# A fused attention and two-layer mixture kernel: where the block means are placed from, which banks the second queries use, and who copies the last transposed weights

## The chip, the cores and the metric

The kernel runs on one core of one Trainium2 chip. The metric is device time in microseconds (us) of one execution. Three runs of the kernel before took 491.3, 493.27 and 496.1 us, the median is 493.27. One execution was profiled.

## The reference, cut to what matters

```python
# q, k, v: (2, 8, 768, 64) float32
block, window = (32, 16)
k_sum = k.reshape(B, H, nb, block, D).max(axis=3)     # 24 block maxima per head
v_sum = v.reshape(B, H, nb, block, D).mean(axis=3)    # 24 block means per head
scores_l = scale * np.matmul(q, k.transpose(0, 1, 3, 2))
scores_s = scale * np.einsum('bhsd,bhnd->bhsn', q, k_sum) + np.log(block)
scores_l_m = np.where(np.abs(pos[:, None] - pos[None, :]) < window, scores_l, -1e9)
a = softmax(np.concatenate([scores_l_m, scores_s], axis=-1))
attn = np.matmul(a, np.concatenate([v, v_sum], axis=2))
x = attn.transpose(0, 2, 1, 3).reshape(B * S, H * D)  # 1536 x 512
h = x @ w_in; x = (h * np.cos(h)) @ w_out             # 512 -> 2048 -> 512
h = x @ w_in2; solu = h * softmax(h)                  # 512 -> 1024
out = layernorm(solu) * g_ln @ w_out2                 # 1024 -> 512
```

## The kernel before, in words

The program has three stages. The first is the attention, some 103 us; the two feed-forward parts follow and are long runs of matmuls. The order of every engine's work is written out by hand: what the Python code emits first runs first on its engine.

The attention goes over 8 pairs of heads, each cut into 3 groups of 4 query tiles, 24 groups in all. `step` counts from 0 to 28, and each stage of a group lags behind the scores: in step s, TensorE makes the scores of group s+1 (`emit_s`, tile `sps`, L510), transposes the softmax weights of group s-4 (`emit_t`, tile `aps`, L547) and multiplies them with the values of group s-5 (`emit_av`, tile `ops`, L565). ScalarE takes the exponential of group s-1 (L530), copies the transposed weights to SBUF (`emit_at`, tile `at`, L555; from group 20 on VectorE does it, L553) and copies the products into `X` (L579; VectorE from group 19, L577). VectorE finds the row maxima (L521) and sums, GpSimd subtracts and normalizes (L525, L540).

For each pair the keys and queries are loaded (`kt`, `qt`), laid side by side (`kg`, `qg`), transposed by TensorE (L443, L482) into one PSUM tile `qk`, and read out: block maxima by VectorE (`ksum`, L455), key windows by ScalarE (`kx`, L464, then the ends, L471 and L474, one step later), scaled queries by ScalarE (`qx`, L496). Pair 0 is different: its queries go into banks 2 and 3 (tiles `q0`, `q1`), which are not yet needed, and VectorE scales them out of there in two halves (L492).

The values of a pair are loaded in four DMAs (`vt`, L389 and L393). The block means are made on the chip: TensorE sums blocks (`sum_v`, tile `vsum`, L421), ScalarE scales the sum (`scale_v`, tile `vm`, L429), and two DMAs place it into rows 96 to 119 of `vt` for all 12 tiles (`place_vsum`, L436). The first product of the pair needs both placings. `VSUM_AT` says in which step a pair's means are summed; the placing is issued a step later, by SyncE (SP), which issues all loads too. Two or three weight tiles of the feed-forward part are prepared during the attention (loads `raw`, L163, L164, L171, L186, L187).

In the program, each DMA takes one of eight completion semaphores, in turn over all issuing engines, and before it is issued it waits for the last transfer that had the same one.

From step 24 on (`drain`), the first hidden tiles of the feed-forward part run through ScalarE and VectorE (L243, L248, L253, L258, L263, L264) between the last groups of the attention. Their products `y` (L276) follow the last `ops`.

Of the kernel before, what the change touches and what calls it, by code (L numbers as in the profile page):

```python
# [34 lines left out]
def fused_kernel(  # L35
# [14 lines left out]
    nc = tc.nc  # L50
# [43 lines left out]
    WSTEPS = (4, 7, 10, 13, 16, 19, 20, 21)  # L94
    XS = (7, 10, 13, 16)
    IDLE = (0, 0, 0)
    DVE_AT = 20
    DVE_X = 19
    DVE_NORM = 99
    LAST = 5  # L100
# [225 lines left out]
    def drain(k):  # L326

        if k == 0:
            table(AF.Sin)
        for stage, at in STAGES:  # L330
            if 0 <= k - at < GF and (stage, k - at) != (emit_g, GF - 1):
                stage(k - at)


    def attention():
        st = ExitStack()
        with st:
# [24 lines left out]
            def load_q(n):  # L362
                q_t[n] = load_heads(q, n, "qt", NR)

            def load_k(n):
                k_t[n] = load_heads(k, n, "kt", 2)
# [17 lines left out]
            def load_v(n):  # L384
                b, hp = divmod(n, NP)
                t = io.tile([P, NT, 2, D], F32, tag="vt", name="vt", bufs=4)
                for j in range(2):
                    o = v[b, 2 * hp + j].offset
                    nc.sync.dma_start(  # L389
                        out=t[0:WIN, 1:NT - 1, j, :],  # L390
                        in_=bass.AP(v.tensor, o + (QT - BAND) * D, [[D, WIN], [QT * D, NT - 2], [1, D]]),
                    )
                    nc.sync.dma_start(  # L393
                        out=t[0:WIN, 0:NT:NT - 1, j, :],
                        in_=bass.AP(v.tensor, o, [[D, WIN], [(S - WIN) * D, 2], [1, D]]),
                    )
                v_t[n] = t
# [29 lines left out]
            def scale_v(n):  # L427
                m = io.tile([P, 2 * D], F32, tag="vm", name="vm")
                nc.scalar.activation(out=m, in_=vs_t[n], func=AF.Copy, scale=1.0 / BLOCK)  # L429
                vs_t[n] = m  # L430

            def place_vsum(n):
                m = vs_t.pop(n)
                for c in range(2):
                    at = WIN + c * NS // 2
                    nc.sync.dma_start(  # L436
                        out=v_t[n][at:at + NS // 2].rearrange("p t j d -> p t (j d)"),
                        in_=m[D * c:D * c + NS // 2].unsqueeze(1).to_broadcast([NS // 2, NT, 2 * D]))

# [35 lines left out]
                    out=kx[:, :, WIN:KW], in_=ks_t.pop(n).unsqueeze(1).to_broadcast([P, NT, NS]), func=AF.Copy)  # L475

            def emit_q(n):
                if n == 0:
                    qk_t["q", n] = bank(2, "q0"), bank(3, "q1")
                t, (a, b) = q_t.pop(n), qk_t["q", n]  # L480
                for c in range(NR):
                    nc.tensor.transpose(  # L482
                        (a, b)[c // (NR // 2)][:, (c % (NR // 2)) * P:(c % (NR // 2) + 1) * P],
                        t[:, c].rearrange("p h d -> p (h d)"), ident)

            def emit_qx(n):
                qx = io.tile([P, S], F32, tag="qx", name="qx")
                rows = qx.rearrange("p (i r) -> p i r", r=NR)
                src = qk_t.pop(("q", n))
                if n == 0:  # L490
                    for r in range(2):
                        nc.vector.tensor_scalar_mul(  # L492
                            rows[:, :, r * NR // 2:(r + 1) * NR // 2],
                            src[r][:, 0:S // 2].rearrange("p (r i) -> p i r", i=P), 0.125)
                else:
                    nc.scalar.activation(  # L496
                        out=rows, in_=strided(src[0], 0, [[1, P], [P, NR]]), func=AF.Copy, scale=0.125)
                kx_t["q", n] = qx
# [50 lines left out]

            def emit_at(G):  # L550
                at = sm_p.tile([KW, NG, P], F32, tag="at", name="at", bufs=2)
                if G >= DVE_AT:
                    nc.vector.tensor_copy(at, at_t[G])  # L553
                else:
                    nc.scalar.activation(out=at, in_=at_t[G], func=AF.Copy)  # L555
                at_t[G] = at

            def emit_av(G):
# [27 lines left out]
            nc.sync.dma_start(out=mask.rearrange("p t k -> p (t k)"), in_=c_mask)  # L586
            load_k(1)
            load_q(1)
            load_k(2)
            load_q(2)  # L590
            load_v(0)
            nc.gpsimd.memset(small, 0.0)
            nc.gpsimd.memset(strip, 0.0)
            warm_up(8)
# [12 lines left out]


            LX, LN, LT, LA = 1, 2, 4, 5
            VSUM_AT = {3: 0, 4: 1, 7: 2, 9: 3, 12: 4, 13: 5, 16: 6, 19: 7}  # L610
            VLOAD_AT = {1: 1, 4: 2, 6: 3, 8: 4, 10: 5, 13: 6, 16: 7}
            for step in range(NGR + LA):
                n, g = divmod(step, GPP)
# [34 lines left out]
                    emit_max(step)  # L648
                if step == 1:
                    emit_ksum(ahead)  # L650
                drain(step - NGR)
                if LT <= step < NGR + LT:
                    emit_at(step - LT)
                weights.finish()
                if summed:
                    emit_norm(step - LN)
# [3 lines left out]
                    emit_kx(ahead)  # L660
                if step == 1:
                    emit_kx_ends(1)
                if step == 0:
                    emit_qx(1)
                if g == 2 and n + 2 < NPAIR:
                    emit_qx(n + 2)
# [13 lines left out]
                    load_q(n + 3)  # L680
                if step in VLOAD_AT:
                    load_v(VLOAD_AT[step])
                if step - 1 in VSUM_AT:
                    place_vsum(VSUM_AT[step - 1])
                if step in VSUM_AT:
                    scale_v(VSUM_AT[step])

    with tc.manual_schedule():

# [300 lines left out]
```

## Time and profile before

| | us |
|---|---|
| runs (3) | 491.3, 493.27, 496.1 |
| the profiled execution | 493.17 |
| its span, first to last instruction | 491.4 |
| TensorE busy | 479.3 (98%) |
| ScalarE busy | 313.6 (64%) |
| VectorE busy | 303.0 (62%) |
| GpSimd busy | 152.6 (31%) |

The profiled execution is 0.1 us off the median of the runs; 1.8 us lie around its span. Shares are means over stages: from 103.5 us to the end TensorE runs without a gap to speak of, and what can change is in front of that.

### The profile page before, as it was taken

Reading aid. Unit: us, or ns where it says so; the run is one execution under the profiler, and the core shown is the slowest. Engines: PE = TensorE matmul, PEld = TensorE weight load, DVE = VectorE, ACT = ScalarE, POOL = GpSimd, SP = SyncE. Lnnn points to the kernel's source line nnn. Section 1 sums busy time; section 2 is a strip of 40 time slices with the busy share of each in tenths; the row PEclk is TensorE's granted clock in tenths of the full one; section 3 lists DMA queues with packets and bytes.
Section 4 is the critical chain, followed back from the end, with each engine's and each line's share of the span. In section 5 each row is a group of like instructions: output and inputs, shape, how many; then the busy total and the mean of one; then the engine's idle time right before and its main releaser. Section 6 shows DMA issues by size and latency. Waiting matters only on the chain.

```text
span 491.4 us, 7884 instructions
## 1 busy us (share of the span) xinstructions
PE 479.3 (98%) x2943; PEld 394.5 (80%) x2943; DVE 303.0 (62%) x666; ACT 313.6 (64%) x539; POOL 152.6 (31%) x146
## 2 busy tenths in 40 slices
PE   8789999899999999999999999999999999999997
PEld 5668887678888888888888888888888888888886
DVE  3668976883445446556474655556477776776661
ACT  3669878756685766556655653788624867777621
POOL 3469977722432222222222220245500011110000
PEclk9889999999999999999999999999999999999999
DMA  8987854201222322332223220220001333223211
GB/s 258 285 199 210 212 135 127 87 2 43 87 85 90 122 88 87 92 122 88 87 91 120 88 86 27 94 96 0 0 2 43 87 90 83 65 64 65 69 40 43
DMA packets 59046, 46.17 MB, mean 94 GB/s; under 512 B 40448, under 2 KB 51328, under 8 KB 59008
## 3 DMA queue, kind: packets, MB, share of 16 engines
q1 hardware_dynamic: 59008, 45.67, 32.4%
q8 instruction: 23, 0.38, 0.3%
q14 instruction: 15, 0.12, 0.1%
HBM read 36.61 MB, written 3.15 MB: 81 GB/s over the span
## 4 chain that ended last, share of the span: by engine, by line
PE 88%; SPq 5%; POOL 2%; DVE 1%; ACT 1%; issue 1%; DMA 1%
PE y L276 27%; PE h L234 25%; PE o L865 13%; PE h L751 13%; PE sps L510 3%; SPq L393 3%; PE ops L565 2%; PE aps L547 2%; PE vsum L421 2%; SPq L357 1%; SPq L389 1%; POOL sm L525 1%; PE tp L799 1%; DMA vt<-vm 1%; POOL sm L540 1%
## 5 line engine op out<-in xcount | busy, mean ns | idle before, releaser
L234 PE MATMUL h<-xs,w 128*128 128x512 f32 x576 | 141.2, 391 | 0.0
L276 PE MATMUL y<-gs,w 128*128 128x512 f32 x576 | 138.1, 389 | 0.0
L276 PEld LDWEIGHTS y<-gs,w 128*128 128x128 f32 x576 | 108.1, 188 | 22.4
L234 PEld LDWEIGHTS h<-xs,w 128*128 128x128 f32 x576 | 107.2, 188 | 21.6
L187 POOL TENSOR_TENSOR w<-s,w 128x512 fp32r<-128x512 f32 x48 | 62.2, 1295 | 164.9 <-ACT w L186 141.9
L243 ACT ACTIVATE r<-h 128x512 int32<-128x512 f32 x48 | 28.7, 597 | 85.9 <-PE h L234 85.9
L248 DVE SCALAR_TENSOR_TENSOR r<-r,h 128x512 f32<-128x512 int32 x48 | 33.0, 687 | 67.4 <-ACT r L243 67.3
L865 PE MATMUL o<-w,ls 128*128 128x512 f32 (+1 forms) x312 | 67.8, 373 | 0.0
L751 PE MATMUL h<-w,xs 128*128 128x512 f32 x288 | 67.6, 390 | 0.0
L171 DVE SCALAR_TENSOR_TENSOR s<-raw 128x512 int32<-128x512 int32 x48 | 37.9, 790 | 44.8 <-ACT raw L164 38.3
L865 PEld LDWEIGHTS o<-w,ls 128*128 128x128 f32 x312 | 55.3, 188 | 10.7 <-DVE ls L841 0.4
L751 PEld LDWEIGHTS h<-w,xs 128*128 128x128 f32 x288 | 53.9, 188 | 11.1
L786 POOL TENSOR_TENSOR st<-st,mhalf 128x1 f32<-128x1 f32 x12 | 6.6, 550 | 110.1 <-DVE st L785 101.7
L204 POOL TENSOR_TENSOR xs<-X,xs 128x512 fp32r<-128x512 f32 x22 | 29.6, 1353 | 32.7 <-ACT xs L203 32.7
L253 ACT ACTIVATE r<-r,half_pi 128x512 f32<-128x512 f32 x48 | 34.5, 718 | 1.3 <-DVE r L248 1.3
L264 DVE TENSOR_TENSOR gs<-h,gs 128x512 fp32r<-128x512 f32 x48 | 32.6, 680 | 4.2 <-ACT gs L263 4.0
L258 DVE TENSOR_TENSOR h<-h,r 128x512 f32<-128x512 f32 x48 | 32.9, 686 | 0.4 <-ACT r L253 0.4
L163 ACT ACTIVATE raw<-raw 128x512 f32<-128x512 f32 x48 | 31.9, 664 | 0.0
L164 ACT ACTIVATE raw<-raw 128x512 int32<-128x512 uint32 x48 | 31.8, 663 | 0.0
L186 ACT ACTIVATE w<-s 128x512 fp32r<-128x512 f32 x48 | 30.1, 626 | 1.2 <-DVE s L171 0.9
L768 ACT ACTIVATE e<-h,st 128x1024 f32<-128x1024 f32 (+1 forms) x13 | 13.6, 1049 | 26.6 <-DVE st L764 23.1
L525 POOL TENSOR_TENSOR sm<-sm,mx 128x480 f32<-128x480 f32 x24 | 26.1, 1090 | 9.8 <-DVE mx L521 9.5
(81 smaller groups left out, 570.3 us busy)
## 6 DMA issues: line engine op xcount, KB each, us to landing
raw<-in_moe_w_in_dram SPq DMA_DIRECT2D x24, 512.0 KB, 3.6
raw<-in_moe_w_out_dram SPq DMA_DIRECT2D x24, 512.0 KB, 3.3
vt<-in_v_dram SPq DMA_DIRECT2D x16, 240.0 KB, 3.5
kt<-in_k_dram SPq DMA_DIRECT2D x8, 384.0 KB
qt<-in_q_dram SPq DMA_DIRECT2D x8, 384.0 KB, 7.7
out_dram<-osb SPq DMA_DIRECT2D x11, 256.0 KB, 2.0
vt<-vm SPq DMA_DIRECT2D x16, 72.0 KB
vt<-in_v_dram SPq DMA_DIRECT2D x16, 48.0 KB, 4.1
```

Of the source, the lines that this page charges most:

```text
L163: nc.scalar.activation(out=hw, in_=hw, func=AF.Prelu, scale=REBIAS, alpha=NEGATIVE)
L164: nc.scalar.activation(out=lw, in_=lw.bitcast(U32), func=AF.Copy, scale=TOP3)
L171: nc.vector.scalar_tensor_tensor(out=self.f32[i], in0=t[:, :, 1], scalar=3, in1=t[:, :, 0], op0=ALU.logical_shift_left, op1=ALU.bitwise_or)
L187: nc.gpsimd.tensor_tensor(out=w[:, 1, :], in0=f, in1=as32(w[:, 0, :]), op=ALU.subtract)
L234: nc.tensor.matmul(h, lhsT=w[:, a, f * P:(f + 1) * P], rhs=xs_of[tb, c][:, b_, :], start=(m == 0), stop=(m == 3 * KC - 1))
L248: nc.vector.scalar_tensor_tensor(out=r, in0=r.bitcast(I32), scalar=TWO_PI, in1=h_of[step], op0=ALU.mult, op1=ALU.subtract)
L253: nc.scalar.activation(out=r, in_=r, func=AF.Sin, scale=-1.0, bias=half_pi)
L258: nc.vector.tensor_tensor(out=h, in0=h, in1=r, op=ALU.mult)
L264: nc.vector.tensor_tensor(out=gs[:, 1, :], in0=r, in1=as32(gs[:, 0, :]), op=ALU.subtract)
L276: nc.tensor.matmul(y[e], lhsT=w[:, a, e * P:(e + 1) * P], rhs=gs[:, b_, :], start=(f == 0 and i == 0), stop=(f == GF - 1 and i == 2))
L751: nc.tensor.matmul(banks[n], lhsT=xs_of[NTB + t // TPB, c][:, a, t0:t0 + P], rhs=weights.done[w2i[c][n]][:, b_, :], start=(m == 0), stop=( ...
L865: nc.tensor.matmul(o, lhsT=ls_of[t][f // 4][:, a, s0:s0 + P], rhs=w[:, b_, cols], start=(f == 0 and i == 0), stop=(f == NF2 - 1 and i == 2))
```

## The change

Three things. The queries of pair 1 go into banks 2 and 3 like those of pair 0, and VectorE scales them. The placing of the block means is issued from ScalarE's queue, right behind the scaling and in the same step; for pair 0 the sum is moved from step 3 to step 1 and its load ahead of the loads of pair 2. In steps 24 to 27 ScalarE copies the transposed weights instead of VectorE, and `emit_at` stands ahead of `drain`.

```diff
@@ -94,7 +94,6 @@
-    DVE_AT = 20
@@ -433,7 +432,7 @@
                 for c in range(2):
                     at = WIN + c * NS // 2
-                    nc.sync.dma_start(
+                    nc.scalar.dma_start(
                         out=v_t[n][at:at + NS // 2].rearrange("p t j d -> p t (j d)"),
@@ -475,7 +474,7 @@
             def emit_q(n):
-                if n == 0:
+                if n < 2:
                     qk_t["q", n] = bank(2, "q0"), bank(3, "q1")
@@ -487,7 +486,7 @@
                 src = qk_t.pop(("q", n))
-                if n == 0:
+                if n < 2:
                     for r in range(2):
@@ -549,10 +548,7 @@
                 at = sm_p.tile([KW, NG, P], F32, tag="at", name="at", bufs=2)
-                if G >= DVE_AT:
-                    nc.vector.tensor_copy(at, at_t[G])
-                else:
-                    nc.scalar.activation(out=at, in_=at_t[G], func=AF.Copy)
+                nc.scalar.activation(out=at, in_=at_t[G], func=AF.Copy)
@@ -586,9 +582,9 @@
             load_k(1)
             load_q(1)
+            load_v(0)
             load_k(2)
             load_q(2)
-            load_v(0)
@@ -607,7 +603,7 @@
-            VSUM_AT = {3: 0, 4: 1, 7: 2, 9: 3, 12: 4, 13: 5, 16: 6, 19: 7}
+            VSUM_AT = {1: 0, 4: 1, 7: 2, 9: 3, 12: 4, 13: 5, 16: 6, 19: 7}
@@ -648,9 +644,9 @@
-                drain(step - NGR)
                 if LT <= step < NGR + LT:
                     emit_at(step - LT)
+                drain(step - NGR)
                 weights.finish()
@@ -660,7 +656,6 @@
                 if step == 1:
                     emit_kx_ends(1)
-                if step == 0:
                     emit_qx(1)
@@ -680,10 +675,9 @@
-                if step - 1 in VSUM_AT:
-                    place_vsum(VSUM_AT[step - 1])
                 if step in VSUM_AT:
                     scale_v(VSUM_AT[step])
+                    place_vsum(VSUM_AT[step])
```

ScalarE's order from step 2 to the start of step 5, before (`sm` is an exponential, in place; `kx`, `qx`, `at` and `vm` as above):

```order
L530 ACTIVATE sm1_98<-sm1_98 128x4x120
L496 ACTIVATE qx_292<-qk_268 128x768
L530 ACTIVATE sm2_99<-sm2_99 128x4x120
L464 ACTIVATE kx_331<-qk_268 128x10x2x48
L429 ACTIVATE vm_333<-vsum_305 128x128
L530 ACTIVATE sm3_100<-sm3_100 128x4x120
L471 ACTIVATE kx_331<-qk_268 128x2x2x48
L474 ACTIVATE kx_331<-ksum_322 128x12x24
L555 ACTIVATE at_374<-aps_344 120x512
L429 ACTIVATE vm_395<-vsum_349 128x128
L530 ACTIVATE sm4_101<-sm4_101 128x4x120
```

And of the change, with what each row waits for (DMAHW is one of the eight semaphores; the last transfer that had DMAHW6 is the load of `kt` of pair 4):

```order
L529 ACTIVATE sm1_98<-sm1_98 128x4x120 [waits Pool_49]
L495 ACTIVATE qx_312<-qk_288 128x768 [waits PE_49]
L529 ACTIVATE sm2_99<-sm2_99 128x4x120 [waits Pool_49]
L463 ACTIVATE kx_338<-qk_288 128x10x2x48 [waits DVE_49]
L529 ACTIVATE sm3_100<-sm3_100 128x4x120 [waits Pool_49]
L470 ACTIVATE kx_338<-qk_288 128x2x2x48
L473 ACTIVATE kx_338<-ksum_329 128x12x24
L551 ACTIVATE at_379<-aps_349 120x512 [waits PE_49]
L428 ACTIVATE vm_398<-vsum_354 128x128 [waits PE_49]
L435 DMA vt_270<-vm_398 12x12x128 [waits DMAHW3_49,Activation_49]
L435 DMA vt_270<-vm_398 12x12x128 [waits DMAHW6_49]
L529 ACTIVATE sm4_101<-sm4_101 128x4x120 [waits Pool_49]
```

The scaling for pair 0 has moved out of this piece into step 1, ahead of the first row. Behind each of the eight scalings stand two DMAs now, and behind them the exponential of the next step.

TensorE's order from step 0 to step 4, before (`qk` by keys `kg` and queries `qg`):

```order
L443 MATMUL qk_209<-ident_73,kg_199 128x128 x6
L482 MATMUL qk_209<-ident_73,qg_207 128x128 x6
L510 MATMUL sps_224<-kx_167,qx_171 64x120 x8
L510 MATMUL sps_259<-kx_242,qx_222 64x120 x8
L443 MATMUL qk_268<-ident_73,kg_246 128x128 x6
L482 MATMUL qk_268<-ident_73,qg_248 128x128 x6
L510 MATMUL sps_296<-kx_242,qx_222 64x120 x8
L421 MATMUL vsum_305<-vt_125,strip_110 64x128 x12
L510 MATMUL sps_335<-kx_242,qx_222 64x120 x8
L547 MATMUL aps_344<-ident_73,sm0_97 120x128 x4
L421 MATMUL vsum_349<-vt_254,strip_110 64x128 x12
```

And of the change:

```order
L442 MATMUL qk_209<-ident_73,kg_199 128x128 x6
L481 MATMUL q0_216<-ident_73,qg_207 128x128 x3
L481 MATMUL q1_217<-ident_73,qg_207 128x128 x3
L509 MATMUL sps_224<-kx_167,qx_171 64x120 x8
L420 MATMUL vsum_233<-vt_121,strip_110 64x128 x12
L509 MATMUL sps_279<-kx_255,qx_259 64x120 x8
L442 MATMUL qk_288<-ident_73,kg_262 128x128 x6
L481 MATMUL qk_288<-ident_73,qg_264 128x128 x6
L509 MATMUL sps_316<-kx_255,qx_259 64x120 x8
L509 MATMUL sps_340<-kx_255,qx_259 64x120 x8
L546 MATMUL aps_349<-ident_73,sm0_97 120x128 x4
L420 MATMUL vsum_354<-vt_270,strip_110 64x128 x12
```

The first block sums stand in front of the fourth scores, and the queries of pair 1 no longer share a tile with its keys.

ScalarE's order in steps 24 to 27, of the change (before, the four `at` rows were VectorE's, and the first `r` stood right behind `small`):

```order
L529 ACTIVATE sm5_102<-sm5_102 128x4x120
L551 ACTIVATE at_1492<-aps_1470 120x512
L321 ACT_TABLE_LOAD
L321 ACTIVATE small_74<-small_74 128x1
L551 ACTIVATE at_1518<-aps_1497 120x512
L242 ACTIVATE r_1520<-h_1015 128x512
L551 ACTIVATE at_1544<-aps_1525 120x512
L252 ACTIVATE r_1520<-r_1520,half_pi_76 128x512
L242 ACTIVATE r_1548<-h_1305 128x512
L262 ACTIVATE gs_1551<-h_1015 128x512
L551 ACTIVATE at_1573<-aps_1555 120x512
```

Two copies now stand ahead of the first `r` or right behind it.

## Rows read from the trace of the kernel before

**Rows 1.** Windows: us, busy of each engine (instructions), granted clock, DMA share, GB/s.

```profile
20.00:25.43 5.43, 5.43 (x86) 4.60 (x84) 5.21 (x21) 3.79 (x10) 3.40 (x4) 0.98 1.07 347
25.43:79.31 53.88, 51.53 (x762) 43.46 (x759) 44.33 (x179) 42.71 (x91) 45.67 (x40) 0.97 0.72 184
103.49:491.00 387.51, 384.71 (x1732) 318.99 (x1728) 225.98 (x375) 241.56 (x397) 82.97 (x70) 1.00 0.24 71
```

**Rows 2.** Chain that ended last: start us, us, what.

```profile
14.41 3.36 SPq L393
...
23.42 2.58 SPq L393
...
27.15 2.90 DMA vt<-vm
```

**Rows 3.** TensorE timeline: start us, us, engine line op tiles [idle before <-releaser].

```profile
15.66 1.04 PE L510 MATMUL sps<-kx,qx 64*64 64x120 f32 x16 [2.54 <-ACT kx L474]
...
17.82 1.49 PE L482 MATMUL qk<-ident,qg 128*128 128x128 f32 x6
...
20.67 1.53 PE L421 MATMUL vsum<-vt,strip 96*64 96x128 f32 x24
22.13 1.04 PE L510 MATMUL sps<-kx,qx 64*64 64x120 f32 x16
...
30.19 0.92 PE L565 MATMUL ops<-at,vt 120*64 120x64 f32 x16 [2.12 <-DMA vt<-vm]
```

**Rows 4.** VectorE and ScalarE timelines in the head, pairs 0 to 2.

```profile
7.66 1.02 DVE L492 TENSOR_SCALAR qx<-q 128x384 f32<-128x384 f32 x2 [0.50 <-PE q L482]
...
9.58 0.84 ACT L373 ACTIVATE qg<-qt 128x768 f32<-128x768 f32 x1 [0.81 <-DMA qt<-in_q_dram]
...
13.03 0.96 DVE L455 TENSOR_REDUCE ksum<-qk 128x24 f32<-128x768 f32 x1 [1.40 <-ACT qx L496]
...
19.34 0.81 ACT L496 ACTIVATE qx<-qk 128x768 f32<-128x768 f32 x1 [3.25 <-PE qk L482]
...
25.26 0.28 ACT L429 ACTIVATE vm<-vsum 128x128 f32<-128x128 f32 x1 [0.57 <-PE vsum L421]
25.43 0.59 ACT L530 ACTIVATE sm<-sm 128x480 f32<-128x480 f32 x1
```

**Rows 5.** Windows around TensorE's two idle stretches (third last number: granted clock).

```profile
18.00:20.00 2.00, 2.00 (x15) 1.67 (x15) 0.00 (x0) 0.66 (x1) 0.49 (x1) 0.50 0.71 163
...
30.00:32.00 2.00, 1.81 (x26) 1.73 (x28) 0.00 (x0) 0.86 (x2) 0.00 (x0) 0.62 0.89 159
32.00:34.00 2.00, 2.00 (x18) 1.36 (x16) 1.74 (x10) 1.23 (x3) 1.18 (x1) 0.53 1.15 225
```

**Rows 6.** Tile vm and kt, min/median/max ns; SyncE timeline of one pair.

```profile
L436 SPq DMA_DIRECT2D vt<-vm x16: 778/786/997, 26.1 to 80.3; - x16
...
L357 SPq DMA_DIRECT2D kt<-in_k_dram x8: 379/438/722, 0.7 to 51.8; - x8
...
40.07 1.66 SPq L436 DMA_DIRECT2D vt<-vm  x2
```

**Rows 7.** ScalarE timeline: waits in the steady part.

```profile
31.14 0.38 ACT L579 ACTIVATE X<-ops 128x256 f32<-128x256 f32 x1 [3.49 <-PE ops L565]
...
79.14 0.28 ACT L429 ACTIVATE vm<-vsum 128x128 f32<-128x128 f32 x1 [0.63 <-PE vsum L421]
...
82.25 0.38 ACT L579 ACTIVATE X<-ops 128x256 f32<-128x256 f32 x1 [0.74 <-PE ops L565]
```

**Rows 8.** Waits (us in total, times, longest us), then timelines of the drain.

```profile
PE aps L547 <- DVE at L553: 1.6, 2, 0.9
...
101.71 0.68 DVE L553 COPY at<-aps 120x512 f32<-120x512 f32 x1
102.31 0.41 DVE L577 COPY X<-ops 128x256 f32<-128x256 f32 x1
...
94.70 0.58 ACT L243 ACTIVATE r<-h 128x512 int32<-128x512 f32 x1
```

## The prediction, made before the changed kernel ran

> **What bounds the kernel now.** I read the windows first. From 103.5 us to the end TensorE is busy 384.7 of 387.5 us at the full granted clock [rows 1]. Nothing of the change lies there, so every microsecond has to come out of the 103.5 us in front, and it counts only as far as the first `y` starts earlier. The chain of waits, read second, is all SyncE in the head: loads being issued, some of them very slowly (3.36 and 2.58 us for one issue), then the placings, and 2.90 us until the needed ones have landed [rows 2]. That landing releases the first product of pair 0: TensorE starts it at 30.19 after 2.12 us of waiting [rows 3]. In the head TensorE waits once more, 2.54 us until 15.66, for the key windows of pair 1 [rows 3]. After each of the two waits the clock falls: granted 0.50 at 18 to 20 us, 0.62 and 0.53 at 30 to 34 us [rows 5], so for most of this time it is the lower of its two levels, 1.2 GHz.
>
> From there to 79.3 us TensorE is busy 51.5 of 53.9 us; ScalarE is busy 42.7, GpSimd 45.7, VectorE 44.3 [rows 1] (the window runs from ScalarE's exponential of group 4 to that of group 19). So TensorE sets the pace there, and ScalarE has 11.2 us of waiting, the largest part for products of TensorE (3.49 us in one place [rows 7]). These 11.2 us are what the new work on ScalarE has to fit into.
>
> **The head, step by step.** (a) The block maxima of pair 1 started at 13.03 after 1.40 us of waiting for ScalarE's `qx`, which reads the same tile [rows 4]. With queries in banks of their own this wait goes: VectorE, free at 11.6, finishes `ksum` at 12.6 (0.96 us, against 14.0). VectorE then pays 1.02 us for the two halves of `qx`, as it did for pair 0 [rows 4]; ScalarE loses one `qx` of 0.81 us. The key windows, which released the scores at 15.66, end some 1.3 us earlier, about 14.3. (b) In front of the fourth scores now stand the block sums, which run from 13.1, where the idle stretch began (15.66 - 2.54), for 1.5 us [rows 3]. So the scores start at 14.6 instead of 15.66, and TensorE's idle stretch is filled. The values of pair 0 must be there by 13.1. They are 0.6 MB (2 x 240 and 2 x 48 KB) and now follow the load of pair 1, of which ScalarE used the last part at 9.6 [rows 4]; at 347 GB/s [rows 1] that is 1.7 us more, at 163 [rows 5] 3.5, so between 11.3 and 13.1. The keys and queries of pair 2 land as much later in exchange, about when VectorE gets to them. (c) ScalarE scales at 14.6 and issues two DMAs. No row shows a DMA issued by ScalarE. The same two on SyncE took 1.66 us, 0.78 to 1.00 each [rows 6]; that is the nearest row, and I take it, with 0.15 us more, since the row behind `vm` no longer starts 0.11 us before its end [rows 4] and the DMA waits for that end: **1.8 us a pair of placings**. The bounds are 0.76 us (two of SyncE's cheapest issue, 0.38 [rows 6]) and 5 us (two of its slow ones [rows 2]). They end at 16.7 and the exponential behind them at 17.3. The next `qx` needs TensorE's queries: 1.0 us of scores, two transposes of 0.75 each (one took 1.49 at half the clock [rows 3]), so 17.1. It starts at 17.3 against 19.34 [rows 4] and is hardly held by the DMAs. (d) Before, the scores of group 5 started 2.8 us after that `qx` and the scaling of pair 1 3.1 us after these scores (19.34, 22.13, 25.26 [rows 3, 4]). Now: 20.1 and 23.2. Then 0.3 us of scaling, 1.8 us of DMAs, and the exponential of group 4 starts at **25.2, before 25.43: -0.2 us**. TensorE reaches the first product near 26 instead of 30.19, since its placing landed long before. TensorE has won 4 us, ScalarE nearly nothing.
>
> **The steady part.** Now ScalarE is behind, and its sum decides. From the exponential at 25.43 to the one at 79.31 it did 42.7 us of work [rows 1, 7]. Six pairs of placings stand in this stretch (pairs 2 to 7): 6 x 1.8 = 10.8. Of the old 11.2 us of waiting I keep 0.8: the waits for products disappear where TensorE is ahead, the 0.63 us for the last block sum [rows 7] stays, since its scores hang on ScalarE's own `qx`. Sum 54.3 against 53.88: **+0.4**. The next wait for a product, 0.74 us at 82.25 [rows 7], absorbs **0.7**, and GpSimd's chain behind it follows ScalarE. Until step 21 that makes -0.2 + 0.4 - 0.7 = -0.5.
>
> **The rest.** SyncE is relieved of 16 issues, which cost nothing: its loads come well ahead of their use after 30 us, so neither that nor their order buys time. Lower bound nothing, upper bound nothing, except for the keys of pair 4, below. In the drain TensorE waited twice for VectorE's copies, 1.6 us in all [rows 8]. These waits go, but the first `r` on ScalarE, at 94.70, then stands behind two copies more (0.6 us each, one of them in a gap), about 1.0 us later. VectorE's `X` hangs on that chain, in whose rounds it saves a copy, 0.60 us from start to start. The last `X` that releases a product starts at 102.31 [rows 8] + 1.0 - 2 x 0.6 + 0.2 of new waiting for ScalarE = 102.3, and the last product follows it as before. I take **-0.15**; the bounds are -1.6 (both waits gone) and +1.0 (the late `r` in full).
>
> **Sum:** -0.5 - 0.15 = -0.65, on 493.17 of the profiled execution, which is 0.1 from the median: **492.5 us**. An exchange, not a gain: 4 us that TensorE wins in the head are spent on 12.6 us of issues on ScalarE.
>
> **The page that disagrees.** The rows say 0.78 us of the issuing engine for one placing. The Trainium skill, "DMA: Bandwidth & Descriptors", gives about 50 ns for the sequencer's part of a DMA (section "Anatomy of one DMA — SWDGE (gpsimd) path", so for another issuing path), and says under "Issuing engines are not separate DMA queues" that issuing is usually small beside the transfer. By it the seven pairs would cost 0.7 us and the time would be that of the first rival. This trace does not agree, with 0.78 us.
>
> **Rivals.**
> 1. *ScalarE hardly pays for the issue.* For it: SyncE issues other DMAs in 0.38 us [rows 6]. Against it: all 16 placings took at least 0.778 there. At 0.76 us a pair the seven after the first are 7 us cheaper, more than TensorE can use: it would be the bound again, with its 4.2 us of earlier start and the 1.7 us that the lower clock cost it after 30.19 (2 x 0.38 + 2 x 0.47 [rows 5]). Time 493.2 - 5.9 = 487.3; with part of it, up to 489.5. Chance 0.2.
> 2. *Slower: the DMA holds ScalarE's queue.* ScalarE works in order, and a DMA that can't go out stops everything behind it. Two things may hold it: the issue itself stalls while loads crowd the engines, as SyncE's did for 3.36 us at 14.41 and 2.58 at 23.42 [rows 2], exactly where the first two placings now stand; or the semaphore's last transfer has not landed, for pair 1 the keys of pair 4, which queue behind two weight tiles. For it: the DMA share is 1.07 at 20 to 25 us [rows 1]. Against it: later placings on SyncE took 1.66 us [rows 6], and the share is 0.72. Price: holding the first two for 2 to 3 us puts the exponential of group 4 to 27 to 29, +2 to +4, so 495 to 497; if later ones are held by 1 us each as well, 500. It decides from the point where a pair costs more than 1.9 us on average: each 0.1 us more is 0.7 us of time. Chance 0.25.
> 3. *The clock falls once more.* In my times TensorE has 1.5 to 2 us of waiting before 20 us, for the maxima. After 2.54 and 2.12 us it fell to 1.2 GHz [rows 3, 5]. At half speed the scores, transposes and sums before the second scaling take 1.5 us longer: 494. Chance 0.2, inside the range.
> 4. *The change doesn't do what it says:* the drain's copies shift the wait to VectorE's `X` and lose up to 1 us, the early sum waits for its load. 493.5; chance 0.1, not told from the forecast.
>
> That leaves 0.25 for the sum as it stands.
>
> **How the numbers follow.** Forecast with cases 3 and 4: 0.55, from 491 to 494.5. Case 1: 487 to 489.5. Case 2: 494.5 to 500. The range 488 to 497.5 leaves out half of case 1 and the far end of case 2. One per cent, about what a measurement of this kernel can tell from no change, is 4.9 us: faster than 488.3 is two thirds of case 1 (0.14), slower than 498.2 a third of case 2 and some unknown (0.11), the rest within.
>
> **What would show it.** In the changed profile: ScalarE's exponential of group 4 near 25.2; the first product near 26 without a wait for `vt<-vm`; gaps of 1.8 us behind seven `vm` rows; ScalarE's waits for `ops` nearly gone until 72 us and TensorE's idle time spread over the steady part instead; the exponential at 79.31 shifted by -0.5 to +1; the last product at 102.7. It is wrong if a pair of issues costs much under 1.5 or over 2.2 us, or if TensorE and not ScalarE still paces the part after 30 us.

## The result and the profile after

The changed kernel takes 496.56 us in the median of 18 runs (494.99 to 499.57), the kernel before, beside it, 493.23 (491.3 to 496.1). The ratio is 1.0072 with a 95% interval of 1.0052 to 1.0092: 0.7% slower, where no change was forecast. The profiled execution took 496.0 us with a span of 494.2; before it was 493.17 and 491.4.

| starts at, us | before | after | difference |
|---|---|---|---|
| exponential of group 4 (ScalarE) | 25.43 | 27.30 | +1.87 |
| exponential of group 19 | 79.31 | 82.73 | +3.42 |
| first `y` (TensorE) | 103.49 | 106.27 | +2.78 |

The 2.78 us are the whole 2.8 by which the span grew (387.9 us lie between the first `y` and the end in both): nothing changed behind the first `y`. The profiled execution lies 0.6 us under the median of the runs. ScalarE's timeline in the head, and around the last pair of placings (start us, us, engine line op tiles [idle before <-releaser]; ACTq is ScalarE's DMA queue being issued):

```profile
14.74 0.28 ACT L428 ACTIVATE vm<-vsum 128x128 f32<-128x128 f32 x1 [0.51 <-PE vsum L420]
15.05 2.23 ACTq L435 DMA_DIRECT2D vt<-vm  x2
17.33 0.60 ACT L529 ACTIVATE sm<-sm 128x480 f32<-128x480 f32 x1 [2.31 <-DMA vt<-vm]
17.84 0.79 ACT L495 ACTIVATE qx<-qk 128x768 f32<-128x768 f32 x1
...
25.32 0.28 ACT L428 ACTIVATE vm<-vsum 128x128 f32<-128x128 f32 x1 [1.48 <-PE vsum L420]
25.63 1.62 ACTq L435 DMA_DIRECT2D vt<-vm  x2
27.30 0.60 ACT L529 ACTIVATE sm<-sm 128x480 f32<-128x480 f32 x1 [1.70 <-DMA vt<-vm]
...
81.06 1.62 ACTq L435 DMA_DIRECT2D vt<-vm  x2
82.73 0.61 ACT L529 ACTIVATE sm<-sm 128x480 f32<-128x480 f32 x1 [1.70 <-DMA vt<-vm]
...
84.83 0.37 ACT L575 ACTIVATE X<-ops 128x256 f32<-128x256 f32 x1
```

Each pair of placings stands alone on ScalarE: 0.31 us after the scaling begins the issue begins, and the exponential behind it starts after 1.7 to 2.0 us without work, 2.31 us at the first pair. The trace names the transfer as releaser, but the exponential reads nothing that it wrote, and it starts 0.05 us after the last issue ends (15.05 + 2.23 and 17.33, 25.63 + 1.62 and 27.30): ScalarE's order held it. The wait of 0.74 us for a product at 82.25 [rows 7] is gone.

What the late exponential at 17.33 does, on VectorE, then on TensorE:

```profile
17.96 0.66 DVE L533 TENSOR_REDUCE ss<-sm 128x4 f32<-128x484 f32 x1 [1.25 <-ACT sm L529]
```

```profile
20.63 1.54 PE L509 MATMUL sps<-kx,qx 64*64 64x120 f32 x16 [2.54 <-DVE mx L520]
22.10 1.11 PE L546 MATMUL aps<-ident,sm 128*120 128x128 f32 x4
23.14 2.13 PE L420 MATMUL vsum<-vt,strip 96*64 96x128 f32 x24
25.20 1.04 PE L509 MATMUL sps<-kx,qx 64*64 64x120 f32 x16
...
28.06 0.69 PE L561 MATMUL ops<-at,vt 120*64 120x64 f32 x16
```

The sum waits for it, the maxima stand behind the sum and the block maxima on VectorE, and TensorE waits 2.54 us for the maxima. The scores, transposes and block sums behind that take 1.54, 1.11 and 2.13 us where they took 1.04, 0.65 and 1.53 at the full clock; the scaling of pair 1 waits for these sums until 25.32. The first product no longer waits for its placing and starts at 28.06 instead of 30.19 [rows 3]. By windows (us, busy time of PE, PEld, DVE, ACT and POOL, granted clock, DMA share, GB/s):

```profile
20.00:22.00 2.00, 1.37 (x16) 1.20 (x16) 1.97 (x17) 1.16 (x2) 1.44 (x2) 0.75 0.97 336
22.00:24.00 2.00, 2.00 (x14) 1.56 (x14) 2.00 (x4) 1.33 (x4) 2.00 (x3) 0.50 1.00 336
24.00:26.00 2.00, 2.00 (x36) 1.83 (x32) 1.69 (x11) 0.28 (x1) 1.20 (x2) 0.90 1.14 335
...
27.30:82.73 55.43, 50.21 (x755) 42.16 (x754) 40.79 (x168) 42.55 (x91) 43.20 (x40) 1.00 0.68 173
82.73:106.27 23.54, 19.93 (x239) 14.72 (x238) 16.19 (x50) 19.74 (x38) 12.47 (x13) 1.00 0.26 74
106.27:494.00 387.73, 384.75 (x1731) 319.03 (x1728) 225.73 (x375) 241.40 (x396) 83.00 (x70) 1.00 0.24 71
```

The stretch between the two exponentials, 53.88 us before [rows 1], takes 55.43, though TensorE has less to do in it at the full clock (the half clock at 30 to 34 us [rows 5] is gone). ScalarE's work is the same, 42.55; its waits between 26 and 80 us (us in total, times, longest us) say where the rest is:

```profile
ACT sm L529 <- POOL xs L203: 5.4, 3, 2.0
ACT sm L529 <- POOL sm L539: 3.4, 2, 1.7
ACT sm L529 <- DMA vt<-vm: 1.7, 1, 1.7
ACT X L575 <- PE ops L561: 0.8, 3, 0.3
```

The first three lines are six pairs, 10.5 us: the releaser is whatever ended last by the profile, but each of the six lies behind an issue of 1.62 to 1.90 us. (This window has pair 1's wait in it and leaves out the last pair's; both are 1.70, so the six pairs between the two exponentials come to 10.5 us as well.) The waits for products, 8.6 us before, are down to 0.8. ScalarE sets the pace now.

### The profile page after: what moved, and what is told of

Read it like the earlier page. It is cut to its first block, busy times and chain, and to the rows that moved or that the text cites. A ratio compares the mean times of both kernels' runs of the same rounds, so it can differ in the third digit from the quotient of the medians.

```text
span 494.2 us, 7882 instructions
## 1 busy us (share of the span) xinstructions
PE 477.2 (97%) x2943; PEld 392.5 (79%) x2943; DVE 299.7 (61%) x664; ACT 314.7 (64%) x542; POOL 150.9 (31%) x146
## 4 chain that ended last, share of the span: by engine, by line
PE 84%; ACT 6%; ACTq 3%; DVE 2%; POOL 2%; issue 1%; DMA 1%; SPq 0%
PE y L275 26%; PE h L233 25%; PE o L859 13%; PE h L745 13%; ACTq L435 3%; PE sps L509 2%; PE vsum L420 2%; ACT sm L529 1%; PE aps L546 1%; ACT at L551 1%; DMA qt<-in_q_dram 1%; PE ops L561 1%; DVE ksum L454 1%; ACT qx L495 1%; DVE sm L520 1%
## 5 line engine op out<-in xcount | busy, mean ns | idle before, releaser
L170 DVE SCALAR_TENSOR_TENSOR s<-raw 128x512 int32<-128x512 int32 x48 | 36.3, 756 | 57.5 <-ACT raw L163 49.6
L509 PE MATMUL sps<-kx,qx 64*64 64x120 f32 x384 | 25.2, 272 | 6.9 <-DVE mx L520 4.7
L762 ACT ACTIVATE e<-h,st 128x1024 f32<-128x1024 f32 (+1 forms) x13 | 13.6, 1049 | 26.6 <-DVE st L758 23.2
```

The costliest lines, as they stand in the source:

```text
L170: nc.vector.scalar_tensor_tensor(out=self.f32[i], in0=t[:, :, 1], scalar=3, in1=t[:, :, 0], op0=ALU.logical_shift_left, op1=ALU.bitwise_or)
L509: nc.tensor.matmul(sps[h, i, :], lhsT=qx[h, t * QT:(t + 1) * QT], rhs=kx[h, t, :], start=True, stop=True)
```

## Experiments

All ratios are against the kernel before, run beside each on the same chip; its median lay between 493.2 and 493.9, so medians of different rows compare to some 0.7 us, and where two intervals overlap the medians alone decide nothing. One execution of each kernel was profiled; where that was the fastest of its kernel's runs and a reading rests on it, the text says so. "Group 4", "group 19" and "`y`" are the starts of the table above, in the profiled execution.

| kernel | median us | ratio, 95% interval | group 4 | group 19 | `y` |
|---|---|---|---|---|---|
| e1_sync_place | 490.82 | 0.9956 (0.9930 to 0.9983) | 24.70 | 76.72 | 101.02 |
| e2_keep_clock | 495.23 | 1.0038 (1.0015 to 1.0060) | 25.81 | 81.42 | 104.96 |
| e3_drain_only | 494.39 | 1.0018 (0.9996 to 1.0040) | 26.87 | 79.05 | 103.35 |
| e5_before_scalar | 494.77 | 1.0024 (1.0006 to 1.0043) | 26.69 | 79.16 | 104.78 |
| e4_later | 493.05 | 0.9987 (0.9965 to 1.0009) | 25.47 | 77.53 | 103.26 |
| e7_sync_clock | 493.77 | 0.9989 (0.9960 to 1.0018) | 24.77 | 79.29 | 103.59 |
| e9_banks_only | 494.49 | 1.0017 (0.9996 to 1.0039) | 22.80 | 78.36 | 102.54 |
| e10_four | 515.83 | one run | 34.45 | 102.47 | 125.99 |
| e12_sync_later | 489.47 | 0.9913 (0.9881 to 0.9944) | 25.60 | 76.83 | 101.14 |
| e14_later_but_last | 491.11 | 0.9956 (0.9930 to 0.9981) | 23.39 | 76.43 | 100.70 |
| e15_head_sync | 499.60 | 1.0114 (1.0073 to 1.0156) | 23.81 | 84.91 | 108.45 |
| e16_old_banks | 492.81 | 0.9993 (0.9959 to 1.0027) | 24.42 | 76.38 | 100.66 |
| e17_head_and_5_sync | 493.80 | 0.9987 (0.9964 to 1.0011) | 23.31 | 78.79 | 102.33 |
| e18_sync_later_clock | 489.90 | 0.9917 (0.9890 to 0.9945) | 23.12 | 75.04 | 99.33 |

### Is it ScalarE's queue?

**e1_sync_place**, the changed kernel with one word undone:

```diff
-                    nc.scalar.dma_start(
+                    nc.sync.dma_start(
```

> The changed kernel, but SyncE's queue issues the placings, in the changed order (right behind the scaling, pair 0 early). Theory A, the placings hold ScalarE (10.8 us of idle time ahead of the exponentials of the steady part, and the 2.31 us ahead of the exponential at 17.33 that makes the maxima, the scores at 20.63 and the clock late): ScalarE's idle time behind placings is gone, TensorE's wait of 2.54 at 20.63 is below 1, the clock does not fall between 21 and 24.4, and y begins 4 to 6 us earlier than 106.27; total 490 to 492.5, at or a little below the kernel before. Rival B, the loss is the order of loads, the banks of the second queries or the drain: 496 to 497, as the changed kernel. Rival C, SyncE now waits for the scaling with the next loads behind it (the loads of keys and queries come late): 493 to 495, with TensorE waits behind kt or qt.

490.82, as theory A had it: 5.7 us less than the changed kernel and 0.4% under the kernel before. The stretch between the exponentials is 52.02 us instead of 55.43. One part fell: TensorE still waits 1.82 us in front of the scores, and the clock still falls, a little later (0.50 from 22 to 24 us).

```profile
20.16 1.04 PE L509 MATMUL sps<-kx,qx 64*64 64x120 f32 x16 [1.82 <-DVE mx L520]
```

**e10_four** takes the suspected price and raises it: the same bytes in four DMAs per pair instead of two.

```diff
-                for c in range(2):
-                    at = WIN + c * NS // 2
+                for c in range(4):
+                    at = WIN + c * NS // 4
...
```

> The changed kernel with each pair's placing cut into four DMAs of 6 rows instead of two of 12: same bytes, same place in ScalarE's order. Theory A, ScalarE is held for as long as its queue issues, and an issue has a price per DMA: four in 3.0 to 3.3 us per pair, exponentials behind them 1.6 us later each, the steady part 62 to 66, total 505 to 510. Rival, the price goes by what a DMA moves (0.80 for 12 rows, so 0.4 for 6): pairs still 1.6 to 1.8, total 496 to 498. Rival, the hold is the landing of the transfer and not the issue: 496 to 498 too, with the exponentials behind the landing, not behind the last issue.

An issue has a price per DMA. ScalarE, at one pair of the steady part:

```profile
44.83 3.13 ACTq L436 DMA_DIRECT2D vt<-vm  x4
48.01 0.60 ACT L530 ACTIVATE sm<-sm 128x480 f32<-128x480 f32 x1 [3.20 <-DMA vt<-vm]
```

3.13 / 4 = 0.78 us each, beside 1.62 / 2 = 0.81 for 12 rows: half the bytes hardly make an issue cheaper. Four of the six pairs of the steady part took 3.13, two 3.61, and the first two pairs 4.97 and 5.16. The total, 515.8, is beyond what was expected: TensorE now waits as well, and its granted clock is 0.73, 0.93 and 0.83 in the three windows of 20 us from 20 to 80.

**e5_before_scalar** puts that one word into the kernel before:

```diff
-                    nc.sync.dma_start(
+                    nc.scalar.dma_start(
```

> The kernel before with one word changed: ScalarE's queue issues the placings, one step after the scaling as before. Theory A, a pair of placings costs ScalarE 1.6 to 2.0 us: ScalarE's own work in the steady part rises by 6 x 1.8 = 10.8 us of 53.88, most of what it idles now (11.2), so that part grows by 1 to 2 us and, with the pairs in the head (0 and 1) on the path of the exponentials, the total by 2 to 4: 495 to 497. Rival, the cost of the change comes from placing in the same step, right behind the scaling (the DMA waits for the scaled row first): a placing issued one step later costs ScalarE 0.1 to 0.3 only, and the total is 493.2 within 0.7. Rival B, the order of loads and banks cost it: 493.2 too, but with 1.6 us and more of idle time behind each pair.

494.77, 0.2% slower and just under what theory A expected. The stretch between the exponentials takes 52.47 us, not 55: the same sixteen DMAs on the same queue hardly hold ScalarE there. The first `y` is 1.3 us later than before all the same; that is lost in the head (26.69 beside 25.43) and behind group 19 (25.62 us beside 24.18). Its timeline at one pair, then at the last one:

```profile
30.40 0.38 ACT L579 ACTIVATE X<-ops 128x256 f32<-128x256 f32 x1 [1.50 <-PE ops L565]
30.47 0.81 ACTq L436 DMA_DIRECT2D vt<-vm  x1
30.68 0.81 ACT L496 ACTIVATE qx<-qk 128x768 f32<-128x768 f32 x1
31.32 0.79 ACTq L436 DMA_DIRECT2D vt<-vm  x1
32.15 0.63 ACT L186 ACTIVATE w<-s 128x512 fp32r<-128x512 f32 x1 [0.66 <-issue]
...
82.10 0.38 ACT L579 ACTIVATE X<-ops 128x256 f32<-128x256 f32 x1 [0.73 <-PE ops L565]
82.16 1.62 ACTq L436 DMA_DIRECT2D vt<-vm  x2
83.83 0.63 ACT L186 ACTIVATE w<-s 128x512 fp32r<-128x512 f32 x1 [1.34 <-DMA vt<-vm]
```

In the program both DMAs stand behind `qx`, yet the first is issued while `X` still runs: ScalarE's queue had handed `X` and `qx` over and went on. So the issues, 30.47 to 32.11, lie beside the two copies until 31.49, and 0.66 us of idle time are left. Behind the last pair, which has no `qx`, it is 1.34. In the changed kernel the DMA needs the row that the scaling just in front of it writes, so nothing can lie beside it.

**e4_later** and **e14_later_but_last** try this on the changed kernel, all pairs on ScalarE one step later, and the last pair on SyncE:

```diff
+                if step - 1 in VSUM_AT:
+                    place_vsum(VSUM_AT[step - 1])
                 if step in VSUM_AT:
                     scale_v(VSUM_AT[step])
-                    place_vsum(VSUM_AT[step])
```

```diff
-                    nc.scalar.dma_start(
+                    (nc.sync if n == NPAIR - 1 else nc.scalar).dma_start(
```

> The changed kernel with the placings one step behind the scaling again, still on ScalarE's queue. Theory A', a placing costs ScalarE its whole 1.62 us and the scaling's tail only where it stands right behind the scaling, because it has to wait for the row and nothing is left running on the engine; one step later its issue runs beside copies that were handed over before it (in the kernel before with only the queue changed ScalarE then idled 0.64 to 0.66 per pair, and the exponentials of groups 4 and 19 stood 52.47 us apart against 55.43): exponential of group 4 at 24.5 to 25, the steady part 52.2 to 52.8, from the exponential of group 19 to y 24.5 to 25.6, total 491 to 493. Theory A as first stated, it costs 1.7 to 2 us per pair wherever it stands: steady part 54.5 to 55.5, total 495 to 497.

> Placings on ScalarE's queue one step behind the scaling (total 493.05, from the exponential of group 19 to y 25.73 us against 23.54 of the changed kernel and 24.30 with SyncE), but that of the last pair on SyncE's. Theory: the last pair has no scaled queries to run beside its issue (ScalarE idles 1.34 us behind it, against 0.64 for the others), and from there on ScalarE is late through the whole drain: that part is back at 24.3 to 24.5 and the total 491.5 to 492.0. Rival, the drain is longer for another reason (the order of its weight tiles): 25.5 to 25.8, total 493.

One pair in e4, then the idle time behind it:

```profile
28.83 0.81 ACTq L435 DMA_DIRECT2D vt<-vm  x1
29.05 0.81 ACT L495 ACTIVATE qx<-qk 128x768 f32<-128x768 f32 x1
...
30.52 0.63 ACT L185 ACTIVATE w<-s 128x512 fp32r<-128x512 f32 x1 [0.66 <-issue]
```

493.05 and 491.11: one step of distance is worth 3.5 us. That the last pair is worth another 1.9 is not settled by the runs, since the two intervals overlap; in the profiles the piece from group 19 to `y` takes 25.73 us, then 24.27. Totals and pieces lie within 0.4 us of what theory A' had; the exponential of group 4 in e4 (25.47) came 0.5 us late. ScalarE placing seven pairs a step later (e14) and SyncE placing all (e1) cannot be told apart: 0.9956 both.

### The half clock in the head

**e2_keep_clock** and **e7_sync_clock**: eight empty matmuls in TensorE's wait, in the changed kernel and in e1.

```diff
+                if step == 4:
+                    warm_up(8)
                 if step + 1 < NGR:
                     emit_s(step + 1)
```

> The changed kernel with eight more empty 128x512 matmuls ahead of the scores of group 5, where TensorE waits 2.54 us (8 took 3.24 at the start, 3 took 0.82). Theory A with the clock as a second cost: the granted clock stays at 1.0 from 21 to 24.4; the scores, the transposes and the sum of pair 1 take 1.0, 0.6 and 1.5 instead of 1.54, 1.11 and 2.13, so vm of pair 1 is 1.4 to 1.7 earlier than 25.32 and the total 495.0 (1.5 below the changed kernel). Rival A2, the clock does not matter for the total because ScalarE is the slower engine behind it anyway (its placings take the same): vm earlier, but the total within 0.5 of 496.6. Rival A3, the clock falls a little later all the same: vm at most 0.5 earlier, 496.6.

> The changed kernel with the placings on SyncE's queue and eight empty matmuls in TensorE's wait of 1.82 us ahead of the scores of group 5. With the placings on SyncE alone the clock was 0.5 from 21.9 to some 25 in the profiled execution. If it stays at 1.0: exponential of group 4 at 23.2 to 23.7 instead of 24.70, total 489.3 to 490.0 against 490.8. Rival, empty matmuls come in the way of the scores (they end after the maxima): no gain, 490.8 to 491.3.

In e2 every window of 2 us until 112 shows a granted clock of 1.00, the exponential of group 4 is 1.5 us earlier, and the total 1.3 lower, 495.23 where 495.0 was expected (its interval overlaps a little with the changed kernel's). e7 missed: the head kept its clock, but the exponential of group 4 came at 24.77, no earlier than e1's 24.70, and the total is 493.77, 3 us above e1's, with runs from 489.17 to 497.51. In its profile TensorE waits later on, for the values of pair 5, and the clock is at 0.50 from 56 to 58 us:

```profile
54.34 2.56 PE L420 MATMUL vsum<-vt,strip 96*64 96x128 f32 x24 [1.54 <-DMA vt<-in_v_dram]
```

**e12_sync_later** (e1 with the order of e4) was to let the loads out first, and **e18_sync_later_clock** adds the eight matmuls to it.

> The changed kernel with the placings on SyncE's queue and one step behind the scaling, as they stood before; banks, early values of pair 0 and drain as changed. Theory: a placing that stands in the scaling's own step holds the loads behind it on SyncE's queue until the scaled row is there (the weight load went out at 44.10 and the values of pair 5 from 45.75 to 50.82 where SyncE placed in the same step; where it did not place at all they went at 38.80 and from 44.42 to 47.83), and TensorE's sum of pair 5 then waits for those values in some executions (1.54 us at 54.34, with the clock at half until 59). One step later the loads go first: no wait of that sum, exponential of group 4 at 24.5 to 25, steady part 51.8 to 52.3, total 490 to 491, with the slowest runs below 494. Rival: the placings come too late for the products (2.12 us ahead of the first ops, as before): 492.5 to 493.5.

> The kernel with the placings on SyncE's queue one step behind the scaling (489.47), and eight empty matmuls in TensorE's wait of 1.77 us ahead of the scores of group 5. Theory: the half clock from 21 to 24.4 goes (in the changed kernel that gave 1.3 us) and, since the sums no longer wait for values, does not come again later: exponential of group 4 at 23.8 to 24.3 instead of 25.60, total 488.0 to 488.8, no run above 491. Rival, the clock falls at another place: as without them, 489.2 to 490, with runs on both sides.

489.47 and 489.90: both beat both kernels, by 0.9% and 0.8% against the kernel before. The wait for the values is gone in e12's profile, but its reason was not the expected one: the values of pair 5 were issued from 45.40 us, in e1 from 45.75. The exponential of group 4 came late in it (25.60, expected 24.5 to 25), behind a fall of the clock to 0.50 from 22 to 24 us. Whether e12 is better than e1 stays open; the intervals overlap. The matmuls in e18 bring nothing more in the median: of the six runs of e12 four had a mean clock of at least 0.999 without them.

### The other parts of the change

**e3_drain_only** and **e9_banks_only** are the kernel before with one part each, **e16_old_banks** is e1 without the banks:

```diff
...
-                drain(step - NGR)
                 if LT <= step < NGR + LT:
                     emit_at(step - LT)
+                drain(step - NGR)
```

```diff
-                if n == 0:
+                if n < 2:
                     qk_t["q", n] = bank(2, "q0"), bank(3, "q1")
...
```

> The kernel before with the last part of the change alone (ScalarE copies the transposed weights in steps 24 to 27 too, ahead of the drain's work). As forecast: -0.15 us, so 493.1 beside 493.2, from the bounds -1.6 to +1.0; the wait of the transposes for VectorE's copy (1.6, 2 and 0.9 in all) goes, one for ScalarE comes. Rival, the drain carries a part of the loss: 494 to 494.5. Rival, it carries a gain that the changed kernel hides (the 23.54 us from the exponential of group 19 to y against 24.18): 492.5 or below.

> The kernel before with the first part of the change alone: the queries of pair 1 in banks 2 and 3, scaled by VectorE. Theory, this part took away TensorE's wait of 2.54 us at 15.66 and with it the half clock from 16.5 to 20.6, and is most of what the changed kernel gains where its placings stand on SyncE (490.8 against 493.2): exponential of group 4 at 23.5 to 25, total 491 to 492.3. Rival, the gain comes from the early load and sum of pair 0's values: here 492.7 to 493.5, and TensorE waits for the placing of pair 0 (1 to 3 us ahead of the first ops). As forecast before the result, this part is worth 0.2 us: 493.0.

> The changed kernel with the placings on SyncE's queue (490.82) and the second queries in their old place, scaled by ScalarE. Theory, the early values of pair 0 take away the wait of 2.12 us for the first placing, and the new banks the wait of 2.54 ahead of the scores of group 2; each alone only uncovers the other (the banks alone: 3.88 us of wait for the placing, no gain): here the wait of 2.54 at about 15.7 and the half clock behind it are back, exponential of group 4 at 25.5 to 26.5, total 492.3 to 493.5. Rival, the early values are the whole gain: 490.5 to 491.3.

The drain is worth nothing measurable; from group 19 to `y` it is 24.30 us beside 24.18, so 0.1 where -0.15 was forecast. The banks alone win 2.6 us until the exponential of group 4 (22.80) and lose most of that at the first product, which stands behind pair 0's placing (the profiled execution, 492.26, is the fastest of the ten):

```profile
29.32 1.12 PE L565 MATMUL ops<-at,vt 120*64 120x64 f32 x16 [3.88 <-DMA vt<-vm]
```

The theory's gain for the banks alone (491 to 492.3) fell; the rival's wait of TensorE for pair 0's placing is what the row shows, 3.88 us where 1 to 3 were expected. e16 lies where it was expected, 2.0 us above e1, but its interval overlaps with e1's and its profile does not have the wait of 2.54 (1.08 instead; at 490.42 it is the fastest of ten runs that reach 496.46), so the share of the banks is not settled.

### Head and steady part apart

**e15_head_sync** and **e17_head_and_5_sync**: the changed kernel with the placings of some pairs on SyncE.

```diff
-                    nc.scalar.dma_start(
+                    (nc.sync if n < 2 else nc.scalar).dma_start(
```

```diff
-                    nc.scalar.dma_start(
+                    (nc.sync if n in (0, 1, 5) else nc.scalar).dma_start(
```

> The changed kernel with the first two pairs' placings on SyncE's queue, the other six right behind the scaling on ScalarE's. Theory, two separate losses: the head (2.6 us later at the exponential of group 4 than with all placings on SyncE) and the steady part (55.43 against 52.02): here exponential of group 4 at 24.5 to 25, steady part 55 to 55.6, total 493.5 to 494.5. Rival, the head's part is given back later, because loads or ScalarE set the pace there: 495.5 to 496.5. Rival, the steady part only is slow because the head made the loads late: steady part 52 to 53, total 491 to 492.

> The changed kernel with the placings of pairs 0, 1 and 5 on SyncE's queue, the other five right behind the scaling on ScalarE's. Theory: with pairs 0 and 1 alone on SyncE (499.6) the first placing of pair 5 stood on ScalarE until 58.46 though its row was ready at 57.02, because by the program it first waits for the transfer that last had its semaphore, the first placing of pair 4; ScalarE then lost 3.44 us at one place, TensorE waited 2.54 and ran at half clock from 64 to 71. Without a wait there on ScalarE: no idle time above 2.4 us on ScalarE, no half clock between 60 and 72, steady part 53.5 to 55 (five pairs fewer one, 1.7 to 2.3 us of ScalarE each), total 493 to 494.5, so head and steady part are separate losses. Rival, the loss of that kernel is not in pair 5's wait but in placings from two queues: 497 to 500 again.

e15 missed everything: 499.60, slower than the changed kernel, though its head is 3.5 us shorter (four runs; the profiled one, 498.17, is the fastest). ScalarE and TensorE around pair 5, and the window behind:

```profile
56.73 0.29 ACT L428 ACTIVATE vm<-vsum 128x128 f32<-128x128 f32 x1
58.46 1.94 ACTq L435 DMA_DIRECT2D vt<-vm  x2
60.45 0.60 ACT L529 ACTIVATE sm<-sm 128x480 f32<-128x480 f32 x1 [3.44 <-POOL sm L539]
...
62.76 0.62 PE L546 MATMUL aps<-ident,sm 128*120 128x128 f32 x4 [2.54 <-ACT at L551]
```

```profile
64.00:72.00 8.00, 7.71 (x80) 6.31 (x79) 6.68 (x31) 5.05 (x11) 6.02 (x6) 0.58 0.03 7
```

The row was ready at 57.02, the issue began at 58.46. By the program pair 5's first placing waits for the transfer that had its semaphore last, here pair 4's first placing, issued at 52.72. The Trainium skill, "DMA: Bandwidth & Descriptors", section "Anatomy of one DMA — SWDGE (gpsimd) path", says that the wait for a semaphore happens on the issuing sequencer before the DMA goes out; the row fits that, with 1.4 us in which ScalarE did nothing, but does not show which semaphore it was. In e17 that pair is SyncE's: no idle time above 2.31 us on ScalarE in the attention's steady part, no half clock, 493.80, all as expected but the length of the steady part (55.48 us, expected 53.5 to 55). So the 5.8 us between e15 and e17 come with pair 5's placing on ScalarE. That it was pair 4's landing, 5.7 us after its issue, and no other transfer that released 58.46 is read from the program, not shown by a run.

By the medians 2.8 us of the changed kernel's total go with pairs 0, 1 and 5 (496.56 to 493.80), 3.0 more with the other five (to 490.82). In e17's profile, the fastest of its ten runs, all of its gain is in the head: the exponential of group 4 is 4.0 us earlier, the first `y` 3.9. One pair fewer in the steady part saved nothing there; ScalarE waits 2.2 us for products in it instead of 0.8.

## Why the prediction was wrong

- **Steps (a) and (b): right.** The fourth scores start at 14.62 without a wait, forecast 14.6.
- **The price of a pair, 1.8 us: right.** Measured 1.62 to 1.90 us of issue in the steady part, 1.7 to 2.0 of idle time; six pairs 10.5 us against 10.8. Rival 1 fell. (The Trainium skill, "DMA: Bandwidth & Descriptors", section "Issuing engines are not separate DMA queues", has issuing as usually small beside the transfer. On ScalarE's queue one issue took 0.79 us for a DMA of 72 KB; the one landing that the rows show took 2.90 [rows 2], so it is not small here.)
- **Step (c), the first pair: too cheap.** 2.23 us instead of 1.66 of issue (1.40 the first of the two, in the chain of waits). That is rival 2, at one pair of the two it named; nothing was held for longer, and every issue began 0.30 to 0.34 us after its scaling began, so no semaphore held a placing in this kernel. That the median lies in rival 2's 495 to 497 is luck: it priced 2 to 3 us of holding at two pairs, and 0.6 was seen at one. That crowding loads slowed this issue is not shown: the DMA share was 1.05 and 1.19 in the windows of 2 us from 14 to 18 us, but 1.14 and 1.09 from 24 to 28 us, where pair 1's issue took 1.62.
- **Step (d) failed.** It put the scores of group 5 at 20.1 and the scaling of pair 1 at 23.2; they came at 20.63 and 25.32. 0.5 us is the first pair, 1.6 the half clock after TensorE's wait of 2.54; with the clock kept, in e2, the exponential of group 4 is 1.5 us earlier. The fall was rival 3, with a chance of 0.2 and counted inside the forecast, although its condition, a wait of 1.5 to 2 us there, was part of the forecast's own times. So the exponential of group 4 came at 27.30, not 25.2, and the first product at 28.06, not near 26: +2.1 of the error.
- **The steady part: +1.1.** 54.3 expected, 55.43 measured. The 0.8 us kept for other waits were too few: there are 2.3 (`X` 0.8, the exponentials, for GpSimd's subtraction, 0.5, the scalings, for the last two block sums, 1.0), so waits for TensorE did not all go. That ScalarE sets the pace and that TensorE's lead is worthless then was right.
- **The 0.7 absorbed at 82.25: right.** The copy at 84.83 starts without a wait.
- **The drain, -0.15: not contradicted.** e3 has +0.1 there, and its total is not told apart from the kernel before.
- **SyncE's relief worth nothing: not contradicted**, since from 8 us to the first `y` TensorE waits for no load before or after. But the other direction was not priced: with the placings left on SyncE the change is 0.4% faster than before (e1), 0.9% with them a step later as well (e12).

The sum was -0.65, the profiled execution +2.8. With the head's 2.1 and the steady part's 1.1 put in it is +2.6. The mechanism, an exchange of TensorE's lead for ScalarE's issues, was the right one; what tipped the balance in the profiled execution were two rivals that were kept apart and came together, a slower first pair, which made TensorE's wait 0.5 us longer, and the fall of the clock behind that wait. That the longer wait caused the fall is not shown: e1 has it after 1.82 us. Nor is the fall the whole miss. The five runs of the changed kernel at a mean clock of 1.000 still took 495.0 to 496.3 us, the four at 0.997, like the profiled one, 496.0 to 496.7. The first pair and the steady part put into the forecast give 494.1, so for the runs without the fall 0.9 us and more stay open.

What the prediction did not see at all is that the price hangs on the place. It took 1.8 us as a cost of the queue; e5 and e4 show that ScalarE pays only what does not lie beside work still running in front of the issue. Right behind the scaling, whose result the DMA reads, that is 1.7 us; a step later it is 0.64 to 0.66 with `X` and `qx` in front, and still 1.34 at the last pair, with `X` alone.

## What to carry to other kernels

A DMA issued from ScalarE's queue cost ScalarE its issue time only as far as no work handed over before it was still running; the other computing engines were not tried. Put such a DMA a step behind the instruction whose result it reads, with long instructions handed over in front of it, or leave it on an idle queue. When a forecast contains a wait of TensorE nearly as long as one that cost the clock elsewhere in the same trace, the lower clock belongs into the sum, with its chance. And of two stalls in a row, price both: in e9, without the wait of 2.54 us, the next one took 3.88 us instead of 2.12.

## What had not been expected of the hardware

- The issue of a placing hardly depends on its bytes on ScalarE's queue: a median of 0.75 us for 6 rows (e10) and 0.79 for 12.
- ScalarE's queue runs ahead of its work: a DMA that stands behind `qx` in the program was issued 0.21 us before `qx` began (30.47 and 30.68 in e5).
- The half clock comes and goes from one execution to the next. After the same wait of 1.82 us near 20 us it came in the profiles of e1 and e4, and not in those of e14, e15, e16 and e17. Of the changed kernel's 18 runs the five with a mean clock of 1.000 took 495.0 to 496.3 us, the two with 0.992 and less 499.1 and 499.6: a spread larger than the change's 3.3 us.
